# PV sums kept feature-major through DRAM instead of being turned twice on TensorE

## The chip, the cores and the metric

The kernel runs on one core of a Trainium2 chip. The metric is the device time of one execution in microseconds. Its matrix engine is TensorE (PE, with weight loads as PEld), its vector engines are VectorE (DVE), ScalarE (ACT) and GpSimd (POOL); SyncE (SP) issues the DMAs. Each engine works through its own queue in order, and waits on semaphores for what others produce.

## What is computed

Two attention branches (A and B) with a compressive memory read the same 2048 tokens of 640 features, and a sigmoid gate per token mixes them. Each has 32 heads of 20 features and works on 4 segments of 512 tokens:

```python
for s in range(N):
    qs, ks, vs = q[:, :, s], k[:, :, s], v[:, :, s]
    logits = jnp.einsum("bhqd,bhkd->bhqk", qs, ks) * scale + mask
    p = _softmax(logits, axis=-1)
    a_dot = jnp.einsum("bhqk,bhkd->bhqd", p, vs)
    pq = phi(qs)
    num = jnp.einsum("bhld,bhde->bhle", pq, M)
    den = jnp.einsum("bhld,bhd->bhl", pq, z)[..., None] + 1e-6
    a_mem = num / den
    o = g * a_mem + (1.0 - g) * a_dot        # g = sigmoid(beta), one per head
    pk = phi(ks)
    M = M + jnp.einsum("bhld,bhle->bhde", pk, vs)
    z = z + jnp.einsum("bhld->bhd", pk)
# each branch: o @ wo; then, with g = sigmoid((x * gate_w).sum(-1)):
return g * a + (1 - g) * b
```

## The kernel before, in words

The work is cut into eight stages `t = 2 * s + b`, one for each segment `s` and branch `b`. What belongs to a stage is "feature-major" when features or heads lie on partitions and the 512 tokens along them, and "token-major" the other way round.

Filler work of a stage are the products `q`, `k`, `v` and `o` (line L690; each one a sum of products of high and low parts, so that fp32r operands give nearly fp32 results; the first two in L736 at full height, the last ones in L1051). The core of the work are 64 units `i = 8 * t + u`, each one a "quad" of four heads. A unit has S products for the row maxima (L1122, reduced by DVE in L1109), the maxima's transposition into rows (L1147), T products (L1212, exponentiated by ACT in L1204 and masked by POOL in L1205), and PV (L1232), which sums over four key blocks into one bank of four times 32 rows: 20 features of a head, the softmax denominator as the 21st row, and unused rows. The eight PSUM banks of [128, 512] are shared by everything; 28 row tiles `row` of [128, 512] in SBUF hold operands and results.

What follows PV is where the change lies. `pv_unit` copies the bank to a row tile `oT` (L1259). `fin_unit` turns it by eight transposes of 64 x 64 (L838, four for each half of the array) to token-major; DVE multiplies the denominators by the gates (L1298, `gq`), takes the reciprocal (L1299) and weighs the features with it (L1300), into `O` or, where the memory part stands there already (stages 2 to 7), into a temporary that POOL adds to `O` (L1310). The memory part comes token-major from `mem_unit` (L800, weighed by DVE in L814 to L817). When all quads of a column block of 128 features are there, `o_transpose` turns `O` back to feature-major by eight transposes (L838), and ACT and DVE split it into high and low parts (L1328, `OTs`), which the `o` products of the stage read. These write partial results through DRAM (`part`) for branch A and the output for branch B. The last stage's output products are split into an early and a last part.

Gates come token-major: `token_gate` sums x times `gate_w` on DVE, `segment_gate` makes sigmoids, and `gates` multiplies them by head factors of beta on POOL into two tiles for each stage, one for the memory part and one for the attention.

The order on every engine is made when the program is built, by a planner in the kernel's own code. It holds a clock for the two 64-row halves of TensorE (`lane`), queues with priorities for the other engines (`put`), and a model of the DMA queue (`dma`). `window_jobs` lists the filler products of a stage; `marks` say how far the filler should be at each unit; `RULES` sets, for a unit, the order of its S and T products and thresholds. A filler product that isn't ready in the plan holds back the ones behind it (`hold_on`); other units go on. x tiles of a new token segment are requested by `want_x`, and the old ones are given back in `used_x` after the 24th product that reads them. After recording, each engine executes its queue as it was recorded.

## Time and profile before

| what | us |
|---|---|
| three runs, median (lowest, highest) | 1026.45 (1025.29, 1026.51) |
| profiled execution, its own time | 1026.22 |
| its span, first to last instruction | 1024.5 |
| busy: PE, DVE, ACT, POOL | 1015.8, 760.0, 659.3, 581.5 |
| bytes of the DMA engines | 207.97 MB |

A row of the groups reads: line, engine, operation, written tile <- read tiles, partitions x elements, count; then busy time in us and mean ns of one; then the idle time of the engine just before them, and what ended it. The same matmul in PV, memory reads and memory updates stands twice in the trace for each once in the program. A row of the chain reads: start, duration, what it was. A row of stretches gives the length, then for PE, PEld, DVE, ACT and POOL the busy time with the count of instructions, then clock, share of the DMA engines and GB/s.

### The profile page before, as it was taken

Reading aid. Unit: us, or ns where it says so; the run is one execution under the profiler, and the core shown is the slowest. Engines: PE = TensorE matmul, PEld = TensorE weight load, DVE = VectorE, ACT = ScalarE, POOL = GpSimd, SP = SyncE. Lnnn points to the kernel's source line nnn. Section 1 sums busy time; section 2 is a strip of 40 time slices with the busy share of each in tenths; the row PEclk is TensorE's granted clock in tenths of the full one; section 3 lists DMA queues with packets and bytes.
Section 4 is the critical chain, followed back from the end, with each engine's and each line's share of the span. In section 5 each row is a group of like instructions: output and inputs, shape, how many; then the busy total and the mean of one; then the engine's idle time right before and its main releaser. Section 6 shows DMA issues by size and latency. Waiting matters only on the chain.

```text
span 1024.5 us, 31917 instructions
## 1 busy us (share of the span) xinstructions
PE 1015.8 (99%) x11780; PEld 873.7 (85%) x11780; DVE 760.0 (74%) x2725; ACT 659.3 (64%) x1337; POOL 581.5 (57%) x1043
## 2 busy tenths in 40 slices
PE   9999999999999999999999999999999999999998
PEld 7988888988988889889898988989889888888876
DVE  4777787678768788676887668967687867778764
ACT  6375777677655675675756458566675656666672
POOL 4364655665444765566646456565774646645561
PEclk9999999999999999999999999999999999999999
DMA  8996866666675676764766468684775865957431
GB/s 274 305 281 186 280 191 211 194 187 219 181 225 163 196 247 197 232 177 145 264 175 221 132 189 276 196 249 140 205 245 157 263 187 164 286 160 225 134 109 53
DMA packets 110028, 207.97 MB, mean 203 GB/s; under 512 B 12464, under 2 KB 16560, under 8 KB 109872
## 3 DMA queue, kind: packets, MB, share of 16 engines
q1 hardware_dynamic: 109872, 205.93, 66.4%
q8 instruction: 93, 1.52, 0.6%
q14 instruction: 63, 0.52, 0.2%
HBM read 131.43 MB, written 73.40 MB: 200 GB/s over the span
## 4 chain that ended last, share of the span: by engine, by line
PE 95%; DMA 2%; DVE 1%; ACT 1%; POOL 0%; issue 0%; SPq 0%; ACTq 0%; DVEq 0%
PE bank L690 54%; PE bank L1232 13%; PE bank L1122 7%; PE bank L1212 7%; PE bank L838 4%; PE bank L800 3%; PE bank L878 3%; DMA qd<-row 2%; PE bank L1147 1%; PE bank L736 1%; PE bank L328 1%; DMA wst<-in_a_wo_dram 1%; PE bank L1051 0%; DVE bank L1109 0%; DVE row L1036 0%
## 5 line engine op out<-in xcount | busy, mean ns | idle before, releaser
L1109 DVE CUSTOM_DVE_ANT_0 bank<-bank,tri 128x256 f32<-128x256 f32 (+3 forms) x1024 | 475.2, 519 | 135.3 <-PE bank L1122 107.6
L690 PE MATMUL bank<-row,wh 64*128 64x512 f32 x2308 | 528.3, 404 | 0.0
L1204 ACT ACTIVATE p<-bank 128x512 f32<-128x512 f32 x596 | 328.7, 601 | 142.0 <-PE bank L1212 110.1
L1205 POOL TENSOR_SCALAR_AFFINE_SELECT p<-p 128x256 f32<-128x256 f32 (+1 forms) x596 | 215.5, 371 | 228.3 <-ACT p L1204 214.7
L690 PEld LDWEIGHTS bank<-row,wh 64*128 64x128 f32 x2308 | 330.0, 186 | 8.9 <-issue 0.6
L690 PE MATMUL bank<-row,wl 64*128 64x512 f32 x1154 | 308.7, 399 | 0.0
L517 POOL TENSOR_TENSOR wl<-wst,wh 128x640 fp32r<-128x640 f32 x115 | 179.8, 1566 | 81.8 <-ACT wh L515 81.0
L690 PE MATMUL bank<-wvh,row 64*128 64x320 f32 x1280 | 198.4, 316 | 0.1
L690 PEld LDWEIGHTS bank<-row,wl 64*128 64x128 f32 x1154 | 180.3, 186 | 4.4
L1122 PE MATMUL bank<-kst,qst 60*128 60x384 f32 (+3 forms) x1024 | 176.8, 318 | 1.3 <-ACT row L1259 0.6
L1212 PE MATMUL bank<-qst,kst 62*128 62x384 f32 (+3 forms) x1024 | 173.1, 318 | 0.2 <-ACT row L854 0.2
L690 PEld LDWEIGHTS bank<-wvh,row 64*128 64x128 f32 x1280 | 161.3, 185 | 3.1 <-issue 1.0
L1232 PE MATMUL bank<-p,vst 128*32 128x512 f32 (+3 forms) x1952 | 148.3, 429 | 0.0
L1109 DVE DVE_READ_ACCUMULATOR2_ANT mx<- 128x1 f32 x1024 | 144.2, 141 | 0.0
L1122 PEld LDWEIGHTS bank<-kst,qst 60*128 60x128 f32 x1024 | 131.1, 185 | 8.6 <-DVE mx L1109 1.3
L1212 PEld LDWEIGHTS bank<-qst,kst 62*128 62x128 f32 x1024 | 128.9, 186 | 6.8 <-DVE mx L1109 1.0
L1232 PEld LDWEIGHTS bank<-p,vst 128*32 128x32 f32 x1952 | 59.3, 109 | 85.1 <-issue 65.3
L515 ACT CAST wh<-wst 128x640 fp32r<-128x640 f32 x119 | 86.4, 743 | 37.6 <-PE bank L690 26.2
L690 PE MATMUL bank<-wvl,row 64*128 64x320 f32 x640 | 109.9, 311 | 0.0
L690 PEld LDWEIGHTS bank<-wvl,row 64*128 64x128 f32 x640 | 87.7, 185 | 0.3
L492 POOL TENSOR_TENSOR wvl<-wst,wvh 128x640 fp32r<-128x640 f32 (+1 forms) x48 | 64.1, 1341 | 17.1 <-ACT wvh L489 16.5
L838 PE MATMUL bank<-ident,row 64*128 64x64 f32 x752 | 72.7, 225 | 0.8 <-ACT row L1204 0.8
(100 smaller groups left out, 1224.5 us busy)
## 6 DMA issues: line engine op xcount, KB each, us to landing
qd<-row SPq DMA_DIRECT2D x120, 256.0 KB
kd<-row SPq DMA_DIRECT2D x120, 256.0 KB
qst<-qd SPq DMA_DIRECT2D x128, 240.0 KB
kst<-kd SPq DMA_DIRECT2D x128, 240.0 KB
wst<-in_a_wq_dram SPq DMA_DIRECT2D x20, 320.0 KB
wst<-in_a_wk_dram SPq DMA_DIRECT2D x20, 320.0 KB
wst<-in_b_wq_dram SPq DMA_DIRECT2D x20, 320.0 KB
wst<-in_b_wk_dram SPq DMA_DIRECT2D x20, 320.0 KB
```

The costliest lines, as they stand in the source:

```text
L492: put("G", 0.77 * n, lambda: nc.gpsimd.tensor_tensor(out=wl[:, a:b, :], in0=w3, in1=r32(wh[:, a:b, :]), op=ALU.subtract), end, prio=4)
L515: put("A", 0.625, lambda: nc.scalar.copy(wh, w3), lambda: put(lo_eng, lo_cost, lambda: lo.tensor_tensor(out=wl, in0=w3, in1=r32(wh), op=AL ...
L517: lambda: lo.tensor_tensor(out=wl, in0=w3, in1=r32(wh), op=ALU.subtract), end, prio=3), prio=6)
L690: return nc.tensor.matmul(bank_of, lhsT=w[ROWS[half]], rhs=x_[ROWS[half]], start=start, stop=stop)
L800: return nc.tensor.matmul(pm[:, a - h0:c - h0, :].rearrange("p h e -> p (h e)"), lhsT=r32(pqTs[t, m][ROWS[half], P * n:P * (n + 1)]), rhs= ...
L838: return nc.tensor.transpose(px[:, n, r], block(n)[r], ident[r, r])
L1109: put("D", w / 960.0 + 0.105, lambda: nc.vector.tensor_tensor_reduce(out=sc[:, off:off + w], in0=sc[:, off:off + w], in1=tri[:, L - w:], s ...
L1122: lane_ops[half].append((mm(w), lambda pair=pair, qb=qb, off=off, w=w, r=r, sc=sc: nc.tensor.matmul(sc[:, off:off + w], lhsT=q[r, pair, P ...
L1204: put("A", 0.483, lambda: nc.scalar.activation(pt, sc, AF.Exp, scale=SCALE), lambda: (bank.give(sc), put("G", 0.15 + 0.105 * len(todo), la ...
L1205: "G", 0.15 + 0.105 * len(todo), lambda: nc.gpsimd.affine_select(out=blocks, in_=blocks, pattern=[[0, len(todo)], [1, P]], base=0, channel ...
L1212: lane_ops[half].append((mm(w), lambda pair=pair, kb=kb, off=off, w=w, r=r, sc=sc: nc.tensor.matmul(sc[:, off:off + w], lhsT=k[r, pair, P ...
L1232: nc.tensor.matmul(po[32 * j:32 * j + 32, P * kb:], lhsT=vst[t % 2][:, kb, h * E1:h * E1 + 32], rhs=pts[i, n, f][0][:, off:off + w], start ...
```

## The change

For stages 0 to 6 PV's sums are no longer turned. `send_dot` writes the 20 feature rows of each head to a DRAM tensor `dots` and the four denominator rows to `dens`, feature-major as they are. When four quads (16 heads) of a stage are there, `reciprocals` loads their denominators as a [128, 64] tile, multiplies them by a beta factor per partition (`gcol`) and by the gates as rows (`row_gate`), takes the reciprocal and writes it back (`recs`); one DMA from DRAM to DRAM spreads each head's row over its 20 features (`wide`). `mix` then loads 128 rows of `dots` and of `wide` and multiplies them on DVE or POOL. Stages 0 and 1 have no memory part, so their product goes straight to the split; for stages 2 to 6 `o_transpose` turns the memory part alone, and DVE adds it. Stage 7 keeps the old way.

The gates as rows come by one transpose for each half of the array and segment (`grow_unit`), through DRAM twice. The beta factor per partition comes from the loaded betas by a sum under a mask `own`. The output products of a stage now come after the first two products of the next stage. The table of rules has new values and an eighth field, the threshold `wait2` for the second halves of transposes.

```diff
     RULES = {
-        0: "TSTSTSTSTS 0.969 2.38 0.27 8 0.0 1.6",
+        0: "STTSTSSTST 0.902 2.38 0.24 8 0.0 0.78 1",
...
     def window_jobs(t):
         got = [(t, kind, m) for kind, m in (TAIL if t else [("q", 1), ("k", 1), ("v", 0), ("q", 2), ("k", 2)] + TAIL[2:])]
+        ahead = [(t + 1, kind, m) for kind, m in HEAD] if t < 7 else []
+        got += ahead[:2]
         if t > 0:
             got += [(t - 1, "o", m) for m in range(KT)]
-        if t < 7:
-            got += [(t + 1, kind, m) for kind, m in HEAD]
+        got += ahead[2:]
         return got
...
+            for g in range(2):
+                nc.vector.tensor_tensor_reduce(
+                    out=bts[b][:, 16 * g:16 * g + 16], in0=bts[b][:, 16 * g:16 * g + 16], in1=own, scale=1.0, scalar=0.0,
+                    op0=ALU.mult, op1=ALU.add, accum_out=gcol[b][:, g:g + 1])
+            over_sigmoid(gcol[b], gcol[b], -1.0)
...
+    def grow_unit(s):
+        b = bank.free.pop(0)
+        cols = gate.rearrange("p s b n -> p (s b n)")
+        ops = [[(TURN, lambda a, z, r=r: nc.tensor.transpose(b[:32, r], cols[r], ident[r, r]))] for r in ROWS]
...
+    def spread(r, t):
+        dma(0.2, lambda: nc.sync.dma_start(
+            out=rows_g[t], in_=rowg[t // 2][NB * (t % 2):NB * (t % 2) + NB, :].rearrange("n p -> (n p)")[None, :].to_broadcast([H // 2, L])), lambda: dma(
+                0.2, lambda: nc.sync.dma_start(out=r, in_=rows_g[t].rearrange("h (a n) -> (h a) n", n=SPAN)),
...
+    def send_dot(i, oT):
+        t, u = divmod(i, 8)
...
+        one = then_all(5, sent)
+        dma(0.1, lambda: nc.sync.dma_start(out=dens[t][4 * u:4 * u + 4, :], in_=oT[DH::32, :]), one, prio=-1)
+        for j in range(4):
+            dma(0.12, lambda j=j: nc.sync.dma_start(
+                out=dots[t][80 * u + DH * j:80 * u + DH * (j + 1), :], in_=oT[32 * j:32 * j + DH, :]), one, prio=-1)
...
+        def work():
+            nc.vector.scalar_tensor_tensor(
+                out=d, in0=d, scalar=gcol[t % 2][:, g:g + 1], in1=row_gate[t], op0=ALU.mult, op1=ALU.mult)
+            nc.vector.reciprocal(d, d)
...
+            dma(1.8, lambda: nc.sync.dma_start(
+                out=wide[t][DH * 16 * g:DH * 16 * (g + 1), :].rearrange("(h e) n -> h e n", e=DH),
+                in_=recs[t][rows, None, :].to_broadcast([16, DH, L])), over, prio=-1)
...
+        landed = then_all(2, lambda: anyof(
+            2, weighed,
+            D=(0.605, lambda: nc.vector.tensor_tensor(out=r32(y), in0=r32(y), in1=r32(r), op=ALU.mult)),
+            G=(1.25, lambda: nc.gpsimd.tensor_tensor(out=r32(y), in0=r32(y), in1=r32(r), op=ALU.mult))))
+        dma(0.7, lambda: nc.sync.dma_start(out=r32(y), in_=dots[t][P * k:P * k + P, :]), landed, prio=0)
+        dma(0.7, lambda: nc.sync.dma_start(out=r32(r), in_=wide[t][P * k:P * k + P, :]), landed, prio=0)
...
+        def add():
+            y = mixed.pop((t, k))
+            put("D", 0.605, lambda: nc.vector.tensor_tensor(
+                out=r32(y), in0=b, in1=r32(y), op=ALU.add), lambda: (bank.give(b), parts()), prio=2)
...
-        if u and next_start(half, u["ops"][half][0][0][1])[1] >= u["at"] + (rule["wait"] if u["turn"] else 0.0):
+        if u and next_start(half, u["ops"][half][0][0][1])[1] >= u["at"] + (rule["wait2"] if u["turn"] else 0.0):
```

How the order changes, at three places. The first is TensorE's queue behind the last PV of stage 1, before; `row17_5609` is the copy of its sums.

```order
L1122 MATMUL bank5_122<-kst2_86,qst2_82 128x512
L690 MATMUL bank3_120<-row15_3043_2668,wh3_134 128x512
L1147 MATMUL bank0_117<-ident_68,mt17_4815 32x64
L838 MATMUL bank7_124<-ident_68,row17_5609_4864 128x64
L690 MATMUL bank3_120<-row26_3093_2719,wh3_134 128x512
L838 MATMUL bank7_124<-ident_68,row17_5609_4864 128x64 x3
```

After the change the same place (behind the same stage's last PV, with the maxima `mt17` again) has products and S and T work alone.

```order
L1207 MATMUL bank3_161<-ident_68,mt17_4704 32x64
L748 MATMUL bank7_165<-row14_3271_2697,wl0_170 128x512
L748 MATMUL bank0_158<-row8_3649_2999,wh3_175 128x512
L748 MATMUL bank7_165<-row2_3276_2700,wl0_170 128x512
L748 MATMUL bank0_158<-row15_3847_3140,wh3_175 128x512
L748 MATMUL bank7_165<-row8_3649_2999,wl0_170 128x512
L1272 MATMUL bank4_162<-qst0_80,kst0_84 128x512
```

The transposes of the sums left TensorE's queue there.

The second place is SP's queue in stage 3, where stage 2's output weights are loaded, before.

```order
L1080 DMA kst3_87<-kd3_108 60x2x512 x2
L523 DMA wst2_127<-in_a_wo_dram 128x640
L670 DMA kd3_108<-row0_8070_6997 128x512 x2
L670 DMA kd3_108<-row8_8071_6998 128x512
L523 DMA wst0_125<-in_a_wo_dram 128x640
L670 DMA qd3_100<-row22_8125_7037 128x512 x2
L670 DMA qd3_100<-row11_8126_7038 128x512
```

And after the change.

```order
L1367 DMA recs2_133<-dn1_192 128x64
L728 DMA kd3_108<-row10_9044_7084 128x512 x2
L728 DMA kd3_108<-row9_9045_7085 128x512
L1372 DMA wide2_140<-recs2_133 320x1x512
L1219 DMA qst2_82<-mr0_189 2x8x128 x2
L728 DMA qd3_100<-row3_9151_7181 128x512 x2
L728 DMA qd3_100<-row1_9152_7182 128x512
L1337 DMA dens3_127<-row23_9175_7213 4x512
L1339 DMA dots3_120<-row23_9175_7213 20x512 x4
L648 DMA rows_g5_154<-rowg2_147 16x512
L546 DMA wst0_166<-in_a_wo_dram 128x640
L1408 DMA row9_9299_7312<-dots2_119 128x512
```

The reciprocals, the spread, the pieces of a PV sum and the loads of both operands now stand among the stores of q and k and the loads of weights.

The third place is TensorE's queue where the last `v` product of stage 3 ends, before; `row5_6438`, `row10_6439` and `row18_7010` are parts of stage 2's mixed result, so these are its output products.

```order
L1212 MATMUL bank5_122<-qst1_81,kst1_85 128x128
L690 MATMUL bank3_120<-row5_6438_5650,wh2_132 128x512
L690 MATMUL bank7_124<-wvl_137,row6_3469_3072 128x320
L690 MATMUL bank7_124<-wvl_137,row12_3601_3178 128x320
L690 MATMUL bank3_120<-row5_6438_5650,wl2_133 128x512
L690 MATMUL bank3_120<-row10_6439_5651,wh2_132 128x512
```

After the change the last `v` product of stage 3 is followed by 88 matmuls that are no products (PV, memory reads, transposes of `O`, memory updates, S and T), and then by the first products of stage 4, which read x tiles of the next token segment (`row16_8914`, `row4_8936`, `row14_9376`, `row11_9380`).

```order
L938 MATMUL bank0_158<-vst1_89,row10_9181_7220 128x147
L938 MATMUL bank3_161<-vst1_89,row21_8483_6676 128x168
L938 MATMUL bank6_164<-vst1_89,row13_8926_7003 128x147 x2
L748 MATMUL bank5_163<-row16_8914_6998,wh0_169 128x512
L938 MATMUL bank6_164<-vst1_89,row13_8926_7003 128x147
L748 MATMUL bank5_163<-row4_8936_7012,wh0_169 128x512
L748 MATMUL bank1_159<-row16_8914_6998,wh3_175 128x512
L748 MATMUL bank5_163<-row14_9376_7379,wh0_169 128x512
```

The output products of stage 2 moved behind those of the next stage's first q and k.

127 lines of the change are left out of this document (105 added, 22 removed), and 117 rows, old and new, of the table RULES.

## The prediction

> **What bounds the kernel.** I read the busy shares first, then the slices, then stretches of 100 us, and last the chain of work that ended last.
>
> ```profile
> span 1024.5 us, 31917 instructions
> PE 1015.8 (99%) x11780; PEld 873.7 (85%) x11780; DVE 760.0 (74%) x2725; ACT 659.3 (64%) x1337; POOL 581.5 (57%) x1043
> PEclk9999999999999999999999999999999999999999
> q1 hardware_dynamic: 109872, 205.93, 66.4%
> by line: PE bank L690 54.1%; PE bank L1232 13.5%; PE bank L1122 7.1%; PE bank L1212 6.9%; PE bank L838 4.4%; PE bank L800 3.1%; PE bank L878 3.0%; DMA qd<-row 1.6%; PE bank L1147 0.8%; PE bank L736 0.7%; PE bank L328 0.6%; DMA wst<-in_a_wo_
> ...
> 0.00:100.00 100.00, 97.67 (x1002) 84.56 (x1004) 67.97 (x233) 57.37 (x116) 50.08 (x84) 1.00 0.86 265
> 100.00:200.00 100.00, 100.00 (x1222) 87.10 (x1222) 74.42 (x273) 71.67 (x148) 60.58 (x116) 1.00 0.73 222
> ```
>
> TensorE is busy for 99% of the span at full clock and nearly all of the chain is its own. DVE at 74%, ACT and POOL have room, the DMA engines (66.4%) too. In the stretch from 100 to 200 us TensorE lost nothing with the DMA engines at 0.73; in the first it lost 2.3 us at 0.86, which also holds the start. So what leaves TensorE leaves the time, unless its in-order queue then waits for something new.
>
> **Transposes.** The order shows the whole of TensorE's change: 752 transposes of rows become 304, 320 of `O` become 240, and 8 of gates come in. 520 fewer of 10,254; the other matmuls stay, only moved. A transpose's own duration is no price, as neighbours overlap; its price is its share of the chain.
>
> ```profile
> L838 PE MATMUL bank<-ident,row 64*128 64x64 f32 x752 | 72.7, 225 | 0.8 <-ACT row L1204 0.8
> L838 PE MATMUL bank<-ident,O 64*128 64x64 f32 x320 | 34.4, 226 | 0.1
> ...
> 1001.24 0.24 PE bank L838 x7
> ...
> 1013.81 0.40 PE bank L838 x4
> 1014.22 0.04 issue
> 1014.26 0.46 PE bank L838 x4
> ```
>
> 4.4% of 1024.5 us is 45.1 us for 752 + 320 = 1,072 transposes, 42 ns each. Seven in a row at 1001 us took 34 ns each, eight alone at the tail 0.90 us, 112 ns each. I take 42, since it is the mean over all those places. 528 x 0.042 = 22.2 us go; the 8 gate transposes are nearest to the maxima's line L1147 (0.8% is 8.2 us for its 128, 64 ns each) and add 0.5 us. Net 21.7 us, between 17.5 (at 34) and 58 (at 112, an end that the packed middle of the kernel does not allow, as 1,072 of them would then be 120 us).
>
> **Vector work** lies beside TensorE and costs nothing as long as no engine becomes the bound.
>
> ```profile
> L1300 DVE TENSOR_TENSOR ft<-bank,fw 128x320 f32<-128x320 f32 x48 | 23.6, 492 | 4.8 <-DVE fw L1299 0.5
> L1299 DVE RECIPROCAL fw<-fw 128x16 f32<-128x16 f32 x64 | 16.2, 253 | 2.5 <-DVE fw L1298 0.4
> L1298 DVE TENSOR_TENSOR fw<-bank,gqd 128x16 f32<-128x16 f32 x64 | 10.9, 171 | 19.7 <-PE bank L838 12.5 <-ACT row L1204 2.9 <-PE bank L1122 1.4
> L1328 DVE TENSOR_TENSOR row<-bank,row 128x512 fp32r<-128x512 f32 x40 | 27.5, 688 | 15.1 <-ACT row L1328 12.4 <-POOL mt L1134 2.6
> L1310 POOL TENSOR_TENSOR O<-O,ft 128x320 f32<-128x320 f32 x46 | 40.9, 890 | 30.9 <-DVE ft L1300 26.7 <-DVE mw L814 4.1
> L535 ACT CAST row<-row 128x512 fp32r<-128x512 f32 x20 | 12.0, 622 | 2.8 <-DMA row<-in_xT_dram 2.5
> L539 POOL TENSOR_TENSOR row<-row,row 128x512 fp32r<-128x512 f32 x15 | 19.3, 1298 | 2.3 <-ACT row L535 2.1
> ```
>
> DVE loses 56 weighings of 492 + 253 + 171 ns, 51 us, and 35 low parts of 688 ns, 24 us. It gains 25 adds (688), 52 of the products and low parts that need no bank (I use 690), and 14 reciprocal pairs on 64 columns, between the rows of 16 (253) and of 512 columns (688), say 0.55 us: 17 + 36 + 8 = 61 us. Net 14 us less. POOL loses 40 adds of 890 ns and 9 gate products, gains 18 of 1,298 ns: 16 us less. ACT's casts only change their source. The gate rows, the beta columns and the masks are a few dozen instructions under a microsecond at the start of each segment; the same idle quarter hides them. The range holds nothing for this part: even 20 us more on DVE would leave it at 77%.
>
> **Bytes and issues.** 224 pieces of 40 KB and 56 of 8 KB go out, 14 spreads write 655 KB each, 70 tiles of 256 KB come back, the rest is small: 37 MB more, so the share rises to about 66.4 x 243/206 = 78% of a like span, some 80% of a shorter one. SP issues 410 more.
>
> ```profile
> L1080 SPq DMA_DIRECT2D qst<-qd x128: 315/371/1831, 19.9 to 964.2; - x128
> L670 SPq DMA_DIRECT2D qd<-row x120: 319/418/1071, 14.7 to 931.4; - x120
> ```
>
> 893 + 410 issues at 0.42 us are 547 us of SP's span: room again, but SP is in order. Each piece of a PV sum stands ahead of loads of quads and weights, and whoever waits for those waits behind it.
>
> **The new round trip.** Before, a PV sum was turned, weighed and turned back within a few microseconds. Now the last sums of a stage take five hops in series: out, denominators in, reciprocals out, spread, both operands in. Only the output products of the stage wait for them, but TensorE's queue is in order, so that wait would hold everything. What a hop costs under load stands in the chain, at the places where it stepped onto a DMA:
>
> ```profile
> 302.05 6.36 DMA qd<-row
> ...
> 554.36 5.97 DMA qd<-row
> ...
> 738.08 4.17 DMA qd<-row
> ...
> 917.41 5.28 DMA wst<-in_a_wo_dram
> ```
>
> Mean 5.45 us for about 256 KB; these are hops that were late, so a usual one is shorter, while the spread moves 2.5 times the bytes. Take 5.45 for each of the five: 27.2 us. Between them stand the copy of the sums (0.6), 14 issues (5.9) and, at 0.55 to 0.69 us, the reciprocal, product, high and low part (2.5): 9.0 us; from stage 2 on also the memory part's transposes and add (1.0). That is 36.2 us, or 37.2.
>
> The cover is TensorE's work between a stage's last PV and its first output product. By the changed order these are 354, 338, 417, 450, 437, 396 and 391 matmuls; before, 10,254 took 1024.5 us, 0.1 us each, so 35.4, 33.8, 41.7, 45.0, 43.7, 39.6 and 39.1 us. The shortfall is 0.8 + 2.4 = 3.2 us in the first two stages and none later. With hops of 4.17 us it is nothing; with 6.36 it is 5.4 + 7.0 + 0.1 + 2.2 + 2.7 = 17.4. I take 3.2.
>
> The Trainium skill, page "DMA: Bandwidth & Descriptors", section "Anatomy of one DMA — SWDGE (gpsimd) path", puts a DMA at 2.0 us plus bytes at 436 GB/s, fitted on another issue path; as an estimate the five hops would then be some 15 us, nothing would fall short, and the sum below would be 1007. The rows above, 4.17 to 6.36 us for what that makes 2.6, do not agree, and they decide.
>
> **Heads ahead of the outputs.** The first two products of the next stage now stand before the five output products. Where a new token segment begins, those heads need new x tiles, which need row tiles that the old x gives back only after its last product. The order has two stretches there without any product, 88 and 71 matmuls long (8.8 and 7.1 us); before, the longest past the start was 37. In such a stretch a tile must land (4.17 to 6.36), be cast (0.62) and have its low part made, three tiles one behind the other on POOL (3 x 1.30): 8.7 to 10.9 us. Shortfall 0 to 2.1 and 1.6 to 3.8 us. Some tiles are asked for earlier, so I take 1 us each, 2 us.
>
> **The table.** The new rows and the second waiting threshold only move instructions within TensorE's queue. I cost them at nothing: the order keeps products between S and T nearly everywhere, and where it does not, the two stretches above carry the price. If that cover is thinner than it looks, the loss belongs to the second rival, if thicker to the first.
>
> **Sum,** against the profiled execution's 1026.22 us (its span plus 1.7): 1026.2 - 22.2 + 0.5 + 3.2 + 2.0 = 1009.7; that execution lies 0.2 us under the median, so 1010. Start, last stage and tail are as before.
>
> **Rivals.** *More than the transposes.* 66 turning units each held one of eight banks and had TensorE's second half wait for the first. If the work around them packs tighter, a transpose was worth more than its share, say 55 ns (a fifth of the way from 42 to 112): 29.0 us go, 1003. For it speaks that S and T products wait for banks; against it, that TensorE shows nearly no idle time to be won:
>
> ```profile
> 309.27 0.50 PE L1122 MATMUL bank<-kst,qst 60*128 60x512 f32 x1 [0.51 <-DVE row L854]
> ```
>
> This is one of the largest stalls of the middle, half a microsecond.
>
> *The cover fails in part.* Hops at 6.36 us and x tiles at the upper shortfall: 1026.2 - 21.7 + 17.4 + 5.9 = 1028; halfway, 1018. For it: 13 points more of DMA share, and SP's order; against it: the first 200 us run at 0.73 and 0.86 without such waits.
>
> *Slower.* The place is the first output product of stages 0 to 6, the price what a hop is longer than its cover allows, five times over. It decides where hops average 6.5 us: the shortfalls then reach the 19.7 us that are left to lose. At 7.0 us they are 8.6 + 10.2 + 3.3 + 1.3 + 5.4 + 5.9 = 34.7 us, and the time is 1041. All four late hops above stayed under 6.4. The same page, section "Latency and other measured facts", gives HBM access 0.2 us on average and 2 us at high load; 1.8 us on each hop would make this case. No row here shows TensorE waiting at such a load, so it stays a rival.
>
> *The change does not remove TensorE time,* because transposes on one half of the array ran beside products on the other: then only the waits are left, 1026 + 0.5 + 5 = 1032. Against it: the chain gives them 45 us of their own.
>
> **Chances.** Forecast, 1005 to 1016: 0.46. More than the transposes, below 1005: 0.20. Cover fails in part, 1016 to 1024: 0.17. No change within 0.2% (2 us either way, about what a measurement of this kernel can tell): 0.04. Slower: 0.13, of which the long hops 0.09 and no TensorE time removed 0.04. Faster is 0.83. From 999 to 1026 us the range holds the first, the third, the fourth and three quarters of the second, 0.82.
>
> **What would show it.** After: 544 transposes of `row` and `O`, about 23 us in the chain; TensorE near 99%; DMA near 80%; DVE 10 to 20 us less. A late round trip shows as TensorE idle at the first products that read mixed rows, released by ACT, DVE or POOL from those rows' lines or by the loads of `dots` and `wide`; late x tiles as idle at the first products of stages 4 and 6, released by POOL's low part. I am wrong if these idle times pass 20 us, or if TensorE's matmuls around the DRAM traffic take longer with no idle shown.

## The result, and the profile after

The change made the kernel slower: 1059.24 us, the median of four runs (1056.41 to 1060.1), against 1025.87 (1024.99 to 1026.51) before. The ratio is 1.0321, with a 95% interval from 1.0299 to 1.0343. The prediction was 1010, with a range from 999 to 1026.

The page of the changed kernel has these lines in answer to those shown of before: the span, the busy time of each engine, the clock in slices, the DMA queue, and the shares of the chain that ended last.

```profile
span 1058.4 us, 31354 instructions
PE 1013.3 (96%) x11260; PEld 853.4 (81%) x11260; DVE 768.8 (73%) x2642; ACT 658.2 (62%) x1338; POOL 582.9 (55%) x1016
PEclk9999999999999999999999999999999999999999
q1 hardware_dynamic: 137152, 244.50, 75.6%
PE 69%; DMA 16%; DVE 4%; ACT 3%; issue 3%; POOL 2%; SPq 2%; DVEq 0%; ACTq 0%; POOLq 0%
```

The last of these lines read so before:

```profile
PE 95%; DMA 2%; DVE 1%; ACT 1%; POOL 0%; issue 0%; SPq 0%; ACTq 0%; DVEq 0%
```

No engine has become the bound, and the DMA engines are at 75.6%, below the 80% that were expected. But TensorE's time without work is now 1058.4 - 1013.3 = 45.1 us, where it was 8.7, and the chain stands on a DMA for 16% of the span instead of 2%. Three stretches of 100 us after the change, with the columns as before, show that the loss is everywhere and not at the seven places where a stage's output products begin. The fourth line is the last of these stretches before the change; the prediction shows the other two:

```profile
0.00:100.00 100.00, 94.32 (x936) 82.01 (x938) 65.30 (x228) 56.88 (x117) 48.51 (x85) 1.00 0.87 265
100.00:200.00 100.00, 93.24 (x1062) 77.38 (x1061) 71.53 (x258) 65.16 (x137) 56.92 (x106) 0.98 0.78 240
400.00:500.00 100.00, 93.55 (x1059) 78.31 (x1059) 75.13 (x249) 59.85 (x122) 56.67 (x95) 1.00 0.77 231
400.00:500.00 100.00, 100.00 (x1158) 86.36 (x1156) 71.29 (x262) 67.69 (x139) 67.00 (x113) 1.00 0.63 193
```

The transposes did go, in the numbers predicted (304 + 240 = 544):

```profile
L898 PE MATMUL bank<-ident,row 64*128 64x64 f32 x304 | 32.4, 226 | 0.0
...
L898 PE MATMUL bank<-ident,O 64*128 64x64 f32 x240 | 19.7, 227 | 0.3
```

The view of waits says who waited for a DMA. A row gives engine, line, what it waited for, and then the us in total, the times and the longest. After the change:

```profile
DVE row L1406 <- DMA row<-wide: 22.9, 18, 3.8
ACT wvh L512 <- DMA wst<-in_b_wv_dram: 18.4, 14, 3.1
ACT row L558 <- DMA row<-in_xT_dram: 15.0, 8, 4.9
DVE dn L1362 <- DMA dn<-dens: 13.6, 11, 4.0
DVE wst L603 <- DMA wst<-in_x_dram: 8.3, 4, 5.5
```

and before, for the same loads of weights and x:

```profile
ACT wvh L489 <- DMA wst<-in_b_wv_dram: 3.7, 6, 1.2
ACT row L535 <- DMA row<-in_xT_dram: 2.5, 3, 1.3
```

Two of the five rows are loads of the new round trip (36.5 us); the other three are old loads, of weights and x, that now come late although nothing about them was changed. All waits of the three vector engines for a DMA sum to 125 us, where they were 31. How such a wait reaches TensorE is seen in the chain and on three queues around 440 us. First the chain:

```profile
438.12 5.06 DMA dn<-dens
443.19 0.02 issue
443.21 0.29 DVE dn L1362
443.50 0.02 issue
443.53 0.05 DVE dn L1364
443.58 0.42 issue
444.00 0.27 DVE bank L1169
```

A load of 32 KB took 5.06 us. DVE stood 4.04 us at its product (L1362), and the S maxima (L1169) stood behind it in DVE's queue. At the same time ScalarE stood for a tile of x, with an exponential (L1264) behind it. ScalarE's timeline (start, duration, line, and in brackets the idle time before it and what ended it):

```profile
440.95 0.62 ACT L558 CAST row<-row 128x512 fp32r<-128x512 f32 x1 [3.25 <-DMA row<-in_xT_dram]
441.48 0.59 ACT L1264 ACTIVATE p<-bank 128x512 f32<-128x512 f32 x1
```

TensorE needs the banks that the maxima and the exponentials free. Its timeline shows both waits, the longer one behind the old load of x and the shorter one behind the new load of denominators:

```profile
442.12 0.50 PE L1182 MATMUL bank<-kst,qst 60*128 60x512 f32 x2 [2.43 <-ACT p L1264]
444.38 0.85 PE L748 MATMUL bank<-wvh,row 64*128 64x320 f32 x7 [0.45 <-DVE mx L1169]
```

SP's timeline at that place (start, time of issue, line, tile) shows how its queue holds loads back:

```profile
437.18 0.89 SPq L568 DMA_DIRECT2D row<-in_xT_dram  x2
438.12 0.42 SPq L1382 DMA_DIRECT2D dn<-dens  x1
438.64 0.55 SPq L648 DMA_DIRECT2D rows_g<-rowg  x1
439.28 0.99 SPq L1140 DMA_DIRECT2D qst<-qd  x2
440.32 0.41 SPq L1140 DMA_DIRECT2D kst<-kd  x1
443.41 0.34 SPq L650 DMA_DIRECT2D rg<-rows_g  x1
443.79 0.43 SPq L1140 DMA_DIRECT2D kst<-kd  x1
444.35 0.34 SPq L1367 DMA_DIRECT2D recs<-dn  x1
```

SP issues without a break up to 440.73 and then does nothing for 2.7 us: the next transfer, `rg<-rows_g`, reads what `rows_g<-rowg` writes, and that one, issued at 438.64, lands at 443.39. A load of keys and the rest of the list stand behind it. So "room" on SP, 599 us of issues in a span of 1058, is not room for a transfer that stands behind another.

There is a second thing in SP's queue that no row of before had shown. The program gives SP's transfers eight completion semaphores in turn, and in both traces no transfer was issued before the one eight places ahead of it had landed: 883 of 883 before, 1,293 of 1,293 after. Eight in flight is all that SP has. I counted the issues that came within 0.15 us of that landing, after SP had stood since the issue before: 23 before, for 12.2 us, and 185 after, for 80.5 us.

### The profile page after: what moved, and what is told of

Same layout as the page of the kernel before. It is cut to its first block, busy times and chain, and to the rows that moved or that the text cites. A ratio compares the mean times of both kernels' runs of the same rounds, so it can differ in the third digit from the quotient of the medians.

```text
span 1058.4 us, 31354 instructions
## 1 busy us (share of the span) xinstructions
PE 1013.3 (96%) x11260; PEld 853.4 (81%) x11260; DVE 768.8 (73%) x2642; ACT 658.2 (62%) x1338; POOL 582.9 (55%) x1016
## 3 DMA queue, kind: packets, MB, share of 16 engines
q1 hardware_dynamic: 137152, 244.50, 75.6%
## 4 chain that ended last, share of the span: by engine, by line
PE 69%; DMA 16%; DVE 4%; ACT 3%; issue 3%; POOL 2%; SPq 2%; DVEq 0%; ACTq 0%; POOLq 0%
PE bank L748 40%; PE bank L1292 10%; PE bank L1182 6%; PE bank L1272 5%; DMA row<-wide 3%; DMA dn<-dens 2%; DMA kd<-row 2%; PE bank L938 2%; PE bank L858 2%; PE bank L898 2%; DMA row<-in_xT_dram 2%; ACT p L1264 1%; DMA qst<-qd 1%; DVE bank L1169 1%; DMA wst<-in_b_wk_dram 1%
## 5 line engine op out<-in xcount | busy, mean ns | idle before, releaser
L1169 DVE CUSTOM_DVE_ANT_0 bank<-bank,tri 128x512 f32<-128x512 f32 (+3 forms) x1024 | 474.4, 520 | 138.2 <-PE bank L1182 117.7
L748 PE MATMUL bank<-row,wh 64*128 64x512 f32 x2308 | 502.6, 403 | 0.1
L1264 ACT ACTIVATE p<-bank 128x512 f32<-128x512 f32 x576 | 316.5, 598 | 133.7 <-PE bank L1272 108.7
L748 PEld LDWEIGHTS bank<-row,wh 64*128 64x128 f32 x2308 | 320.7, 186 | 13.8 <-issue 1.2
L748 PE MATMUL bank<-row,wl 64*128 64x512 f32 x1154 | 297.1, 401 | 0.0
L748 PE MATMUL bank<-wvh,row 64*128 64x320 f32 x1280 | 188.5, 316 | 0.9 <-DVE mx L1169 0.4
L1272 PE MATMUL bank<-qst,kst 62*128 62x512 f32 (+3 forms) x1024 | 174.6, 318 | 14.8 <-DVE mx L1169 5.2
L748 PEld LDWEIGHTS bank<-wvh,row 64*128 64x128 f32 x1280 | 154.0, 186 | 4.8 <-ACT p L1264 1.1
L1292 PE MATMUL bank<-p,vst 128*32 128x256 f32 (+3 forms) x1908 | 144.6, 426 | 1.8 <-DVE mx L1169 1.4
L1169 DVE DVE_READ_ACCUMULATOR2_ANT mx<- 128x1 f32 x1024 | 144.7, 141 | 0.0
L715 DVE TENSOR_TENSOR row<-bank,row 128x512 fp32r<-128x512 f32 x80 | 54.3, 686 | 28.2 <-ACT row L708 14.4
```

What stands on the lines that cost most here:

```text
L715: put("D", 0.605, lambda: nc.vector.tensor_tensor(out=lo, in0=src, in1=r32(hi), op=ALU.subtract), out, prio=1)
L748: return nc.tensor.matmul(bank_of, lhsT=w[ROWS[half]], rhs=x_[ROWS[half]], start=start, stop=stop)
L1169: put("D", w / 960.0 + 0.105, lambda: nc.vector.tensor_tensor_reduce(out=sc[:, off:off + w], in0=sc[:, off:off + w], in1=tri[:, L - w:], s ...
L1264: put("A", 0.483, lambda: nc.scalar.activation(pt, sc, AF.Exp, scale=SCALE), lambda: (bank.give(sc), put("G", 0.15 + 0.105 * len(todo), la ...
L1272: lane_ops[half].append((mm(w), lambda pair=pair, kb=kb, off=off, w=w, r=r, sc=sc: nc.tensor.matmul(sc[:, off:off + w], lhsT=k[r, pair, P ...
L1292: nc.tensor.matmul(po[32 * j:32 * j + 32, P * kb:], lhsT=vst[t % 2][:, kb, h * E1:h * E1 + 32], rhs=pts[i, n, f][0][:, off:off + w], start ...
```

## Experiments

Theory A: the round trip is longer than its cover, as in the prediction's rivals. Theory B: the 37 MB more on the DMA engines slow everything. Theory C: the number of transfers on SP is what costs, through its in-order queue and its eight places. Theory D: the transposes were never worth 42 ns. Theory E: TensorE's new order is at fault. Each ratio below is against runs of the kernel before on the same chip.

### The price of a transpose

Of the kernel before, three of the four transposes of each half were left out in stages 1 to 6, 288 in all, with every other instruction of TensorE in its place (on DVE a multiplication with an addition stands in for the reciprocals there); and in another kernel 448 were issued twice.

```diff
-            nc.vector.reciprocal(w, w)
+            (nc.vector.reciprocal(w, w) if t in (0, 7) else nc.vector.tensor_scalar(w, w, 0.0, 1.0, op0=ALU.mult, op1=ALU.add))
...
-        return split_unit(*turn(pxf, lambda n: r32(oT[:, P * n:P * (n + 1)])), take)
+        ops = turn(pxf, lambda n: r32(oT[:, P * n:P * (n + 1)]))
+        if 0 < t < 7:                                  # fewer
+            for half in ops:
+                for n in range(3):
+                    half[n] = (TURN, lambda a, z: None)
+        if t < 7:                                      # twice, in the other kernel
+            ops = [[(TURN, lambda a, z, f=f: (f(a, z), f(a, z))[1]) for _, f in half] for half in ops]
+        return split_unit(*ops, take)
```

> The kernel before, with three of four transposes in each half of the array left out when the PV sums of stages 1 to 6 are turned (288 of 1,072 transposes; what they would have written is stale, and the weights there are set to one). Everything else stands in the same order. If a transpose was worth the 42 ns that the chain gave it, 12.1 us go: 1014 us, between 1010 and 1018. If transposes ran beside other work for nothing, the time stays within 2 us of 1026.

> The kernel before, with each transpose of the PV sums of stages 0 to 6 issued twice in place (448 more). At 42 ns each 18.8 us come on top: 1045 us, between 1040 and 1050. If transposes are free beside other work, 1026 to 1030.

With 448 more: 1045.48 us against 1026.24, ratio 1.0186 (1.0171 to 1.0201), 43 ns each. With 288 fewer: 1028.85 us, ratio 1.0030 (1.0013 to 1.0047), so nothing came back. The reciprocals are replaced in the kernel with fewer alone. Its page:

```profile
PE 1015.7 (99%) x11492; PEld 865.4 (84%) x11492; DVE 768.3 (75%) x2725; ACT 660.0 (64%) x1337; POOL 580.9 (57%) x1043
```

TensorE is as busy as before (1015.8) with 288 instructions less. Its matmuls, matched one by one with those of before, stand 2.3 us later at 380 us and 2.2 us later at 400 us, while twelve transposes between the two points are gone: the time does not come back at the place itself. A part of this is the stand-in's own: it took 378 ns on DVE where the reciprocal took 253, and TensorE stood 3.2 us for the weighted features behind it (L1300), which it never did before. These 3.2 us are far less than the 12.1 expected. So the price is right for what is added, and this order, made with the transposes in it, did not give it back when they were taken out. That the matmuls of the other half of the array set the pace there is the likely reason, and is not shown. Theory D is neither confirmed nor out at this point.

### The round trip without its wait

All transfers of the changed kernel stay, but the loads of denominators and of spread reciprocals read the input, so that they wait for nothing of the round trip (the loads of the sums still read `dots`).

```diff
-            out=d, in_=dens[t][rows, :].rearrange("h (a n) -> (h a) n", n=SPAN)), landed, prio=-1)
+            out=d, in_=xT[4 * g:4 * g + 4, :].rearrange("h (a n) -> (h a) n", n=SPAN)), landed, prio=-1)
...
-        dma(0.7, lambda: nc.sync.dma_start(out=r32(r), in_=wide[t][P * k:P * k + P, :]), landed, prio=0)
+        dma(0.7, lambda: nc.sync.dma_start(out=r32(r), in_=xT[P * k:P * k + P, :L]), landed, prio=0)
```

> The changed kernel in the same order, with the same DMAs in size and number, but the loads of denominators and of spread reciprocals read input tensors that have been there from the start (so the result is left wrong in the weights). Theory A, that the vector engines' in-order queues stand at the heads that wait for the late round trip (43 us of vector idle time behind the loads of wide and dens in the changed kernel's trace): at least half of the loss of 55 us against the expected 1004 comes back, 1030 us, between 1020 and 1040. Theory B, that the added traffic and SP issues make every transfer late: within 6 us of 1059.

1062.32 us, ratio 1.0342 (1.0323 to 1.0362). Theory A falls: with the chain of hops cut, nothing is gained. DVE still stands at the same two lines:

```profile
DVE row L1406 <- DMA row<-in_xT_dram: 23.6, 17, 3.2
DVE dn L1362 <- DMA dn<-in_xT_dram: 11.2, 9, 2.8
```

That is 34.8 us, against 36.5 with the round trip whole. So these loads come late without any hop before them.

### The traffic alone

The kernel before, with the change's pieces and spreads issued at the same places and ten copies of 256 KB from DRAM to DRAM in each stage in place of its loads. Nobody waits for what they bring.

```diff
                 oTs[i] = oT
+                if t < 7:
+                    nc.sync.dma_start(out=dens[t][4 * u:4 * u + 4, :], in_=oT[DH::32, :])
+                    for j in range(4):
+                        nc.sync.dma_start(out=dots[t][80 * u + DH * j:80 * u + DH * (j + 1), :], in_=oT[32 * j:32 * j + DH, :])
+                    if u % 4 == 3:
+                        h = 16 * (u // 4)
+                        nc.sync.dma_start(
+                            out=wide[t][DH * h:DH * (h + 16), :].rearrange("(h e) n -> h e n", e=DH),
+                            in_=xT[h:h + 16, None, :L].to_broadcast([16, DH, L]))
+                if 1 <= t and u < 5:
+                    for c, src in enumerate((xT[P * u:P * u + P, L:2 * L], xT[P * u:P * u + P, 2 * L:3 * L])):
+                        nc.sync.dma_start(out=back[t - 1][P * u:P * u + P, c, :], in_=src)
```

> The kernel before, with the changed kernel's traffic added and nobody waiting for it: the pieces of the PV sums and their denominators written to DRAM, spreads of the same size from an input, and for the loads ten copies of 256 KB per stage from DRAM to DRAM. Theory A: such traffic is hidden, 1026 to 1032 us. Theory B: it costs most of what the changed kernel lost, 1045 us or more.

1126.63 us, ratio 1.0970 (1.0938 to 1.1001): more than the change itself costs, with the DMA engines at 72.6%. So transfers nobody waits for are enough. They were put into an order that has no places for them, so the size is not the change's. A part of it is TensorE's granted clock, 0.970 in the mean of the profiled run (0.999 before, 0.997 in the change): in this trace the clock stood at half in eleven pieces of 3.4 or 6.8 us, 68.3 us in all, and in the 6.8 us ahead of each TensorE had been idle for 1.1 us or more. That makes at most 34 us of the 100 (in the change two pieces, 6.8 us, so at most 3.4). The run leaves B and C, which the next kernels part.

### Many small transfers, and few large ones

The kernel before with 280 transfers at the places of the pieces, but of 16 columns each; and the traffic kernel above with one transfer of 256 KB for a unit in place of its five.

```diff
+                if t < 7:                              # small pieces
+                    nc.sync.dma_start(out=dens[t][4 * u:4 * u + 4, :16], in_=oT[DH::32, :16])
+                    for j in range(4):
+                        nc.sync.dma_start(out=dots[t][80 * u + DH * j:80 * u + DH * (j + 1), :16], in_=oT[32 * j:32 * j + DH, :16])
```

```diff
-                    nc.sync.dma_start(out=dens[t][4 * u:4 * u + 4, :], in_=oT[DH::32, :])
-                    for j in range(4):
-                        nc.sync.dma_start(out=dots[t][80 * u + DH * j:80 * u + DH * (j + 1), :], in_=oT[32 * j:32 * j + DH, :])
+                    nc.sync.dma_start(out=dots[t][P * u:P * u + P, :], in_=oT)
```

> The kernel before, with 280 more transfers of 16 columns alone (1.3 KB to 5 KB... at most 5 KB each) at the places where the changed kernel writes its dots and denominators, from the same tiles; nobody waits for them and they add about 0.3 MB. Theory C (the number of transfers on SP's one queue is what costs: its issue time, and places for transfers in flight): most of the loss without the bytes, 1045 us or more. Theory B (the bytes, 37 MB more on the same 16 DMA engines, are what costs): within 4 us of before, 1022 to 1030.

> The traffic experiment (1126.6) with one transfer of 256 KB for each unit in place of five: 224 fewer transfers, and somewhat more bytes (14.7 MB in place of 9.6 MB for these). Theory C: 1126.6 falls by more than half of its 100 us, to under 1075. Theory B: no lower than 1115.

The small pieces: 1043.68 us, ratio 1.0176 (1.0149 to 1.0202), so 17.8 us for 280 transfers that move 0.3 MB. The DMA share is even lower than before, and the waits for weights and x are back, as the page and the view of waits show:

```profile
q1 hardware_dynamic: 117040, 206.24, 65.4%
```

```profile
ACT wvh L491 <- DMA wst<-in_b_wv_dram: 10.1, 7, 2.5
ACT row L537 <- DMA row<-in_xT_dram: 8.8, 6, 4.0
```

SP stood 38.9 us for its eighth place (12.2 before). The whole units: 1095.74 us, ratio 1.0670 (1.0617 to 1.0722); 224 transfers fewer, with 5 MB more, take 31 us off. That is between the two expectations: with 224 of the traffic kernel's 364 added transfers a third of its loss went, and 140 large transfers with nobody waiting still cost 70 us in this order (at most 31 of them by the clock, 0.972). The count matters and is not all.

### The pieces on another queue

The changed kernel with the 280 pieces issued by ScalarE, and by GpSimd, in the same order.

```diff
-        dma(0.1, lambda: nc.sync.dma_start(out=dens[t][4 * u:4 * u + 4, :], in_=oT[DH::32, :]), one, prio=-1)
+        dma(0.1, lambda: nc.gpsimd.dma_start(out=dens[t][4 * u:4 * u + 4, :], in_=oT[DH::32, :]), one, prio=-1)
         for j in range(4):
-            dma(0.12, lambda j=j: nc.sync.dma_start(
+            dma(0.12, lambda j=j: nc.gpsimd.dma_start(
```

> The changed kernel with its 280 transfers of dots and denominators issued by ScalarE instead of SP, in the same order and with the same bytes. If SP's issue time and its in-order queue are what costs (theory C, its first half): 1040 or less. If it is the places in flight or the bytes, which ScalarE's transfers take as SP's do: 1050 to 1070, and some more where ScalarE loses time to the issues.

> The changed kernel with its 280 transfers of dots and denominators issued by GpSimd instead of SP, which have places of their own in flight. Theory C in either half: 1015 to 1040. Theory B: 1050 to 1065. Slower than the changed kernel if GpSimd's own time for each issue (its engine is 55% busy) holds up the maps and the weighting that it does for the softmax.

From ScalarE: 1090.52 us, ratio 1.0625 (1.0594 to 1.0656), worse by 31 us. Its 280 issues take 105 us of ScalarE's time, and they share the eight semaphores with SP's: ScalarE stood some 47 us for a place, at 76 of them, with the exponentials behind. The granted clock fell to 0.981, which is at most 17 us of the 31. From GpSimd, which has semaphores of its own: 1038.76 us, ratio 1.0132 (1.0115 to 1.0149). With the same bytes and the same order 20.5 us come back, although GpSimd pays for it, as the page shows (q0 is its queue):

```profile
PE 1008.6 (97%) x11260; PEld 853.4 (82%) x11260; DVE 775.7 (75%) x2642; ACT 657.8 (63%) x1338; POOL 720.6 (70%) x1296
q1 hardware_dynamic: 129984, 234.86, 73.4%
q0 software_dynamic: 8960, 9.67, 3.3%
L1339 POOL DMA_DIRECT2D dots<-row x224 | 114.7, 515 | 5.0 <-issue 5.0
```

The Trainium skill, page "DMA: Bandwidth & Descriptors", section "Issuing engines are not separate DMA queues", says that issuing from several engines saves only the sequencer's time, which is usually small beside the transfer. Here it was worth 2% of the kernel. SP's issues took 481 us in place of 599, and what stood behind the pieces came sooner: ScalarE's waits for the loads of branch B's `wv` and of x fell from 18.4 and 15.0 us to 10.8 and 12.9.

### Taking the transfers out of the changed kernel

Its own order, first without the 280 pieces (the loads read the input), then without 406 of its 410 added transfers (the engines do their work on a resident tile).

```diff
-        dma(0.1, lambda: nc.sync.dma_start(out=dens[t][4 * u:4 * u + 4, :], in_=oT[DH::32, :]), one, prio=-1)
+        dma(0.1, lambda: None, one, prio=-1)
         for j in range(4):
-            dma(0.12, lambda j=j: nc.sync.dma_start(
-                out=dots[t][80 * u + DH * j:80 * u + DH * (j + 1), :], in_=oT[32 * j:32 * j + DH, :]), one, prio=-1)
+            dma(0.12, lambda: None, one, prio=-1)
```

> The changed kernel in its own order, with the 280 transfers of dots and denominators left out (weighting reads the input's columns instead; the sums it makes are not the reference's). The rest of the round trip stays: spreads, reciprocals, the wide rows and 70 loads of 256 KB. If these 280 on SP's queue cost what the GpSimd run gave back: 1036 to 1042. If what matters beside them is their 9.6 MB: below 1030. If neither: 1055.

> The changed kernel in its own order with all 406 transfers of the round trip left out, from the pieces to the 70 loads (DVE and GpSimd do all their work on a resident tile instead; the sums are not the reference's). If the transfers are the whole loss and the 520 transposes less are worth what the prediction said: 1002 to 1012. If TensorE's removed time does not come back even without them (as in the run with fewer transposes of the kernel before), or the new order is at fault: 1020 to 1032.

Without the pieces: 1025.56 us, ratio 0.9995 (0.9975 to 1.0015). Without nearly all: 1007.38 us, ratio 0.9815 (0.9792 to 0.9837).

The page of the second:

```profile
span 1004.6 us, 30713 instructions
PE 995.4 (99%) x11260; PEld 850.8 (85%) x11260; DVE 764.4 (76%) x2642; ACT 655.8 (65%) x1338; POOL 585.8 (58%) x1016
```

This settles the main question. On the work of TensorE and the vector engines alone the change gains 1026.2 - 1007.4 = 18.8 us. That is 36 ns for each of the 520 transposes if all of it is theirs; the table, the place of the output products and the vector work differ as well, and no run parts them. So theory D falls where the order is made without them, and theory E falls for the change's own order. The transfers take it back and more, 51.9 us: TensorE stands idle for 35.9 us more (45.1 against 9.2) and is busy for 17.9 us longer with the same 11,260 matmuls (1013.3 against 995.4). By their number it is 18.2 us for 126 of them (1007.4 to 1025.6), 33.7 us for the 280 pieces (1025.6 to 1059.2). Of these 33.7, GpSimd's queue gave 20.5 back. The other 13.2 are the pieces' 9.7 MB, for which the expectation had named a time below 1030 without them, or the 138 us that GpSimd is busier there (720.6 against 582.9); no run parts the two.

### Another order for the same transfers

The planner was told of the eight places and of later landings (the hops' `lat` 1.8 in place of 1.1), and the table was chosen anew for that.

```diff
+        if e == "S" and len(flight) >= 8 and flight[-8] > clk[0]:
+            if not held[0]:
+                held[0] = True
+                at(flight[-8], resume)
+            return
```

> The changed kernel with all its transfers and all its work, in another order: the planner is told that only eight of SP's transfers are in flight at once and that a hop of the round trip lands 0.7 us later than it thought, and the table of rules is chosen anew for that. If the loss is one of an order made for transfers that land on time: at least half of the 33 us come back, 1022 to 1042. If the transfers on SP's queue cost their time in any order: 1050 or more.

1068.68 us, ratio 1.0401 (1.0372 to 1.0429). SP stood 76.3 us for its places, as in the change (80.5). This does not show that the transfers cost as much in any order, since a table found in this way loses time of its own, as the next kernels show.

### Fewer transfers

A version of the change with 123 added transfers. A unit's bank leaves in one transfer of 256 KB; a tile that comes back holds four features of all 32 heads, with the rows of the output weights laid out to match (a second copy of branch B's in the old layout serves stage 7), so that one tile of reciprocals serves five tiles, and nothing is spread in DRAM. Its order was chosen as in the run above.

```diff
-        one = then_all(5, sent)
...
+        dma(0.7, lambda: nc.sync.dma_start(out=dots[t][P * u:P * u + P, :], in_=oT), sent, prio=-1, lat=2.2)
...
+            dma(0.7, lambda: nc.sync.dma_start(
+                out=r32(r), in_=recs[t][:, None, :].to_broadcast([H, EH, L])), r_there, prio=0, lat=2.2)
...
-        dma(0.7, lambda: nc.sync.dma_start(out=r32(y), in_=dots[t][P * k:P * k + P, :]), landed, prio=0)
-        dma(0.7, lambda: nc.sync.dma_start(out=r32(r), in_=wide[t][P * k:P * k + P, :]), landed, prio=0)
+        dma(0.7, lambda: nc.sync.dma_start(out=r32(y), in_=by_head[t][:, EH * k:EH * k + EH, :]), landed, prio=0, lat=2.2)
+        when_r(landed)
```

> The change with fewer transfers: a unit's bank goes out as one transfer of 256 KB, the tiles that come back hold four features of all 32 heads in place of whole heads (rows of the output weights are laid out to match), so one tile of reciprocals serves all five and nothing is spread in DRAM; 123 more transfers than before the change, where the change had 410, and the order chosen as in the run beside it. If the number of transfers on SP is what costs: 286 fewer at the 34 us that 280 pieces cost take most of the loss away, and with the new order the time lies below the kernel before, 1008 to 1024. If the bytes and the round trip cost by themselves: 1030 or more.

1028.39 us, ratio 1.0021 (0.9998 to 1.0043): 31 us better than the change, and level with the kernel before. Its page:

```profile
span 1023.3 us, 30894 instructions
PE 1008.9 (99%) x11260; PEld 859.7 (84%) x11260; DVE 760.6 (74%) x2617; ACT 654.8 (64%) x1337; POOL 593.2 (58%) x1024
q1 hardware_dynamic: 127072, 233.02, 73.5%
PE 88%; DVE 6%; DMA 2%; issue 1%; ACT 1%; SPq 0%; POOL 0%; DVEq 0%; ACTq 0%; POOLq 0%
```

DMA is 2% of the chain again, with the DMA engines at 73.5%, two points below the change's 75.6. That speaks against bytes as the main cost, and so does the change without its pieces, 34 us faster at 75.0%. But TensorE is busy for 1008.9 us with the same 11,260 matmuls that took 995.4 in the change's own order without transfers. Four more kernels asked what holds it: without its transfers; with the wait for its round trip cut; with the sums loaded while the reciprocals are made; and that one with the units issued by GpSimd. The last two have tables of their own.

> The version with tiles of four features of all heads, in its own order, with 119 of its 123 added transfers left out (the engines do their work on a resident tile; the sums are not the reference's). If its transfers cost by the piece as the change's did (34 us for 280, so 14 us for 119): 1012 to 1017. If this order on TensorE is itself no better than before: 1024 to 1029.

> The same version with every transfer in place, but the loads of denominators, reciprocals and sums read the input instead, so that nothing waits for the round trip (the sums are not the reference's). If what is left is the wait for the round trip: 1012 to 1020. If it is the transfers' own cost on SP: 1025 to 1030.

> The same version with the tiles of sums loaded while the reciprocals are still made, so that a single load stands at the end of the round trip, and the order chosen anew. If the round trip's wait is what is left: 1014 to 1023. If not: 1025 to 1032.

> The last with its 56 transfers of whole units issued by GpSimd, so that SP has 67 more transfers than before the change, and the order chosen for that. If the number of transfers on SP is what is left: 1008 to 1020, below the kernel before. If the bytes or the wait: 1024 or more.

Without transfers: 1024.50 us, ratio 0.9980 (0.9970 to 0.9989). So its 119 transfers cost only 4 us, and 17 us lie in the version's own work and order. With the wait cut: 1030.65, ratio 1.0050 (1.0029 to 1.0071), so the wait costs nothing here either. With early sums: 1041.84, ratio 1.0154 (1.0123 to 1.0185). With GpSimd: 1036.31, ratio 1.0102 (1.0086 to 1.0119). The first of these two lies above both of its expectations, the second in its second (1024 or more), and since each has a table of its own they do not say whether their idea or their table is at fault.

The last two kernels tried the version of 1028.39 in another order, made like the change's without a limit on transfers in flight, with and without its transfers.

> The version with tiles of four features of all heads again, the same work and the same 123 added transfers from SP, in another order: the table of rules chosen anew in a planner without the limit of eight transfers, as the change's own order was made. If the order of TensorE's work was what the version lost (its run without transfers stood at 1024.5): below the kernel before, 1010 to 1022. If an order that packs TensorE more tightly only meets later transfers: 1025 to 1035.

> The version in the other order (1034.2) with 119 of its 123 added transfers left out, and their work done on a resident tile (the sums are not the reference's). If the transfers are what holds this order: 1008 to 1016, some 20 us or more below. If the order is: 1026 or more.

1034.19 us, ratio 1.0077 (1.0044 to 1.0109); without its transfers 1025.14, ratio 0.9990 (0.9977 to 1.0004), between its two expectations and near the second. Two orders of this version without transfers stand at 1024.5 and 1025.1, against 1007.4 of the change. Whether that is the table, or that this version must have all heads of a stage before its first tile and then does five products in a row, stays open. No kernel here that does all of the work beats the one before.

The runs side by side; the third column counts SP's transfers, the fourth is the time that SP stood until its eighth place landed, the fifth the span less TensorE's busy time:

| kernel | us | transfers of SP | stood, us | TensorE not busy, us |
|---|---|---|---|---|
| before | 1026 | 891 | 12.2 | 8.7 |
| after | 1059.2 | 1301 | 80.5 | 45.1 |
| before, small pieces | 1043.7 | 1171 | 38.9 | 20.9 |
| before, traffic | 1126.6 | 1255 | 65.8 | 75.9 |
| before, traffic in whole units | 1095.7 | 1031 | 45.2 | 54.5 |
| after, pieces from GpSimd | 1038.8 | 1021 | 37.2 | 27.9 |
| after, no pieces | 1025.6 | 1021 | 44.4 | 18.5 |
| after, no transfers | 1007.4 | 895 | 21.6 | 9.2 |
| four features of all heads | 1028.4 | 1014 | 20.3 | 14.4 |

The time SP stands goes with TensorE's lost time, but not in proportion. SP's issue time grew as well, from 413 us to 599, and which of the two weighs more was not separated: the limit of eight could not be varied by itself. Two more things left SP's queue with the pieces and are not separated either. At the first piece of a unit (L1337) SP stood 57.8 us in all for ScalarE, which makes most copies of the sums. And a piece is another kind of transfer: in the trace its semaphore is raised 11 times (20 rows) or 5 times (4 rows), where that of a transfer of 128 rows, and of the same pieces from GpSimd, is raised 16 times. The small pieces have this form too; 280 small transfers of 128 rows would tell.

## Why the prediction was wrong, step by step

**Transposes.** Right in size, as far as the runs part it. Net 21.7 us less, with 2.0 us for the x tiles on the other side, makes 19.7; the change's order without its transfers gave 18.8. The price from the share of the chain (42 ns) was 43 when transposes were added. What it lacked is that it holds for an order that is made without them: taken out of the order of before they gave nothing back.

**Vector work.** Costed at nothing, which held. Its sizes were off: DVE rose by 8.8 us where 14 less was worked out, POOL by 1.4 where 16 less was. Of DVE's 23 us of error 14 are two terms: its 52 products and low parts that need no bank took 855 and 872 ns (690 was used), and a reciprocal pair took 0.94 us (0.55 was).

**Bytes and issues.** This is the step that failed. It counted 410 more issues, 547 us of SP's span (599 was measured, at 0.46 us each), and gave them no price: "room again, but SP is in order". (The trace before has 891 issues, not 893.) The price was 52 us: 33.7 for the 280 pieces and 18.2 for the rest. The sentence behind it, that whoever waits for loads of quads and weights waits behind the pieces, named the mechanism and was not turned into a term. Instead the allowance for a busier DMA was argued from its share ("13 points more"), and that share came out lower than predicted (75.6%, not 80). Here SP's queue, with 57% of the span in issues and eight places in flight, delayed what stood in it while the DMA engines were a quarter idle.

**The round trip.** Costed at 3.2 us; cutting its wait gained nothing (1062.3 against 1059.2). The hops were shorter than the 5.45 us taken: from issue to landing the medians in the changed kernel are 3.4 (denominators out), 3.2 (in), 3.3 (reciprocals out), 5.5 (spread) and 4.5 (operands in), 19.9 us together against 27.2. The Trainium skill, page "DMA: Bandwidth & Descriptors", section "Anatomy of one DMA — SWDGE (gpsimd) path", makes 12.3 us of five hops of 8, 32, 32, 640 and 256 KB, as an estimate, not the prediction's some 15; that is short by 7.6, and the trace lies between the two. What was not looked for is that DVE stands at `dn` and at `row` for 36.5 us (L1362, L1406), with the S maxima behind it. With the round trip cut it stood there for 34.8, so that is the lateness of SP's transfers again and not the length of the trip.

**What would show it.** The idle time was expected at the first products that read mixed rows. It lies in all stretches of the kernel, and ahead of the S and T products, as the last numbers of these rows of the changed kernel's page show:

```profile
L748 PE MATMUL bank<-row,wh 64*128 64x512 f32 x2308 | 502.6, 403 | 0.1
L1182 PE MATMUL bank<-kst,qst 60*128 60x384 f32 (+3 forms) x1024 | 178.3, 320 | 14.7 <-ACT p L1264 5.3
L1272 PE MATMUL bank<-qst,kst 62*128 62x512 f32 (+3 forms) x1024 | 174.6, 318 | 14.8 <-DVE mx L1169 5.2
```

So the first sign, 20 us of idle time at those products, did not come, although TensorE's idle time as a whole passed it by far.

**The rivals.** The case "Slower" had the right side and the wrong place: it asked for hops of 6.5 us and for TensorE to wait at seven places. No case priced the transfers for those who were there before them, and so 1059 lay outside the range by 33 us.

**The sum by what was measured:** 1026.2 - 18.8 + 18.2 + 33.7 = 1059.3. It closes because each term is the difference of two runs; the terms hold for this order and for leaving the transfers out in this sequence.

## What to carry to other kernels

Price a transfer that is added to an in-order queue by what stands behind it, even if nobody waits for it and it moves next to nothing: 280 of them with 0.3 MB in all cost 17.8 us here, and 280 of 40 KB and 8 KB cost 33.7. When work leaves TensorE, ask whether the order is made anew without it: 288 transposes taken out of a fixed order gave nothing back, a new order with 520 fewer gave 18.8 us without its transfers. Count the transfers of a layout before its bytes: the round trip with 123 in place of 410, in an order of its own, was 31 us faster.

## What the runs showed of the hardware and the program that was not expected

- The program's eight completion semaphores bound SP's transfers in flight: none of 1,293 was issued before the one eight places ahead had landed. ScalarE's transfers take the same eight (the kernel with ScalarE's issues was 31 us slower than the change), GpSimd's take eight others (20.5 us faster).
- An issue takes 0.46 us on SP, 0.37 on ScalarE (105 us for 280) and 0.52 to 0.61 on GpSimd.
- A load of 32 KB took 5.06 us in a stretch with a DMA share of 0.77, longer than most of 256 KB (4.5 by the median of 390).
- TensorE's granted clock stood at half for 3.4 or 6.8 us at a time behind idle time of a microsecond or more: eleven times in the traffic kernel, ten with ScalarE's issues, twice in the change, and never in the kernel before.
